# An attention and MoE kernel on one core: two key chunks loaded uncast and summed by VectorE, a second buffer for turned pooled keys, and new lists of chunks that VectorE evaluates

## The chip, the cores and the metric

The kernel runs on one core of one Trainium2 chip. The metric is device time in microseconds, the median of several runs. Inside a core, TensorE (PE; its weight loads are a row of their own, PEld), ScalarE (ACT), VectorE (DVE), GpSimd (POOL) and SyncE (SP) work side by side, each through its own queue in order.

## The reference

```python
def _attn_ref(q, kv, w_sr):          # q (4, 12288, 128), kv (4, 384, 32, 128), w_sr (128, 128)
    B, N, C = q.shape
    r = 4
    kv_pool = kv.reshape(B, H // r, r, W // r, r, C).mean(axis=(2, 4))
    k = v = kv_pool.reshape(B, -1, C) @ w_sr          # 768 keys per batch
    s = (1.0 / np.sqrt(C)) * (q @ k.transpose(0, 2, 1))
    a = np.exp(s - s.max(-1, keepdims=True))
    a /= a.sum(-1, keepdims=True) + 1e-09
    return a @ v

def _moe_ref(x, w_in, w_out):        # x is the attention's output, (49152, 128); d_ff = 2048
    h = x @ w_in
    g = h * (1.0 / (1.0 + np.exp(-1.702 * h)))
    return g @ w_out
```

Pixels are averaged over 4 by 4 blocks, which gives 768 pooled pixels per batch; keys and values are the same matrix.

## The kernel before

**Tiling.** Queries are taken in 96 blocks of 512 (`G`); 24 blocks belong to a batch. The 768 keys of a batch are 6 chunks of 128 (`JC`); `d_ff` is 16 chunks of 128 (`FCH`). The work has two rounds (`R = 2`): attention for blocks 0 to 47, the MoE layer for them, then both for blocks 48 to 95.

**A chunk's way.** TensorE makes one chunk of scores or hidden values, 128 x 512, in a PSUM bank (`fill_attn`, L357; `fill_moe`, L617). ScalarE evaluates two or three such chunks, a frame, in one instruction (exponential L359, GELU L619) and writes bfloat16 into the ring `ag`, which holds 102 chunks. TensorE takes them up again: in attention as weights against the values (`drain_attn`, L370, 129 columns, four tiles of 128 queries for each chunk), in the MoE layer with `w_out` (`drain_moe`, L627). VectorE then empties the bank: it divides by the row sum (L393, L396) or transposes the output (L638), which SyncE stores from one of three `o_sb` buffers.

**Chunks by VectorE.** For some chunks VectorE evaluates the function with a polynomial, in small steps between its other work: `rolling` names chunks of the exponential (`early_exp`), `lent` chunks of the GELU (`lent_gelu`), and blocks 48 to 51 (`early`) are done so wholly. `rolling` and `lent` results go into a ring of three chunks, `aside`.

**Keys.** For batches 0 and 1, a chunk of pixels is 128 rows of 16 pixels by 128 channels. `load_chunk` loads it through GpSimd, which casts float32 to bfloat16 on the way; the first chunk of batch 0 alone is loaded uncast by SyncE and cast by engines. `pool_chunk` adds the pixels on TensorE: the pixels are the weights, and `sum4`, a 128 x 32 matrix of ones, adds four rows; 4 groups of 4 pixels make 16 matmuls of 32 columns (L141). VectorE copies the result to `pTc` (L144). `key_and_value` makes keys and values from it (L163, L164), and VectorE copies both (L165, L166). Batch 1 is loaded in blocks 10 and 12 of attention and pooled at the blocks that `SUM` names. For batches 2 and 3 GpSimd adds the pixels by accumulating DMAs into `kvs` (`add_kv`, L175), VectorE adds the last two (`sum_kv`, L181), and SyncE brings the transposed result from DRAM into `pT` (`turn_pooled`, L188) for `make_k` (L203).

**Order.** The whole instruction order is written by a planner in the kernel's source, before anything runs: the loop at the end of the function keeps an estimate of TensorE's time (`now`), of VectorE's (`dve`) and of ScalarE's (`end`), in units of one 512-column matmul, and takes at each point a fill, a small job from `extras`, a step of a VectorE chain (`early_step`) or a drain. `COST` holds for each job TensorE's time and the time until its bank is free, `COPY` VectorE's time, `SMALL` the time of one 129-column matmul. Three PSUM banks (5, 6, 7) rotate for everything but the frames. `x` holds 12 tiles of 2048 columns; attention's output goes there, and before it the query and key chunks being loaded (`x_tile`). `gate` makes GpSimd's queue wait until VectorE has come to the same place, which times the loads.

Of the kernel before, what the change touches and what calls it, by code (L numbers as in the profile page):

```python
# [7 lines left out]
F32 = mybir.dt.float32  # L8
F32R = mybir.dt.float32r
I32 = mybir.dt.int32  # L10
BF = mybir.dt.bfloat16
AF = mybir.ActivationFunctionType
AX = mybir.AxisListType
ADD = mybir.AluOpType.add
# [10 lines left out]
def kernel(  # L25
    ctx, tc, q, kv, w_sr, moe_w_in, moe_w_out, out,
):
    nc = tc.nc
    B, N, C = q.shape
    _, H, W, _ = kv.shape  # L30
    r = 4
    Hp, Wp = H // r, W // r
    J = Hp * Wp
    JC = J // 128
    d_ff = moe_w_in.shape[1]
    FCH = d_ff // 128
# [25 lines left out]
    XS = NS // R  # L62
    EARLY = 4
    AG = 102

# [21 lines left out]
    def acc(key=None):  # L87

        nonlocal last_acc
        last_acc = next_acc()  # L90
        turns.append(last_acc)
        turns.remove(last_acc)
        if key:
            closes[last_acc] = key
        return banks[:, last_acc, :]
# [17 lines left out]
    def x_tile(s):  # L113
        return x[:, s % XS * SG:(s % XS + 1) * SG]
# [4 lines left out]
    h = J // 2  # L119
    kv_tiles, kv_sums, pooled, pTs, kTs, vs = {}, {}, {}, {}, {}, {}  # L120

# [6 lines left out]
    def load_chunk(b, jc):  # L128

        a, ch = divmod(jc, HC)  # L130
        t = x_tile(XS - 1 - jc)
        nc.gpsimd.dma_start(out=t, in_=kv_r[b, a, ch])
        kv_tiles[b, jc] = t.rearrange("p (wp w1 c) -> p w1 wp c", w1=r, c=C)

    def pool_chunk(b, jc):

        ps = acc()
        t = kv_tiles.pop((b, jc))
        for wp in (0, 2, 1, 3) if (b, jc) == (0, 0) else range(4):
            for w in range(r):  # L140
                nc.tensor.matmul(ps[:, 32 * wp:32 * wp + 32], t[:, w, wp, :], sum4,  # L141
                                 start=(w == 0), stop=(w == r - 1))
        pTs[b, jc] = kvtmp.tile([128, 128], BF, name="pTc", bufs=2)
        nc.vector.tensor_copy(pTs[b, jc], ps[:, 0:128])  # L144
# [25 lines left out]
    def add_kv(b, n):  # L170
        i, w = divmod(n, r)
        if n == 0:
            kv_sums[b] = kvsum.tile([Hp, 2, Wp, C], F32, name="kvs")
        for i2 in range(2):
            nc.gpsimd.dma_start(out=kv_sums[b][:, i2], in_=kv_p[b, i, w, :, i2],  # L175
                                **({"accum_op": ADD} if n else {}))
# [9 lines left out]
    def turn_pooled(b, a):  # L186
        pTs[b, a] = kvtmp.tile([128, 1, h], BF, name="pT")
        nc.sync.dma_start_transpose(out=pTs[b, a], in_=pool_bf[b, a].rearrange("w h c -> (w h) c"))  # L188
# [64 lines left out]
    nc.sync.dma_start(out=first_f, in_=kv_r[0, 0, 0])  # L253
    w_sr_f = cpool.tile([128, C], F32)
    nc.sync.dma_start(out=w_sr_f, in_=w_sr)
# [47 lines left out]

    w_in_sb = cpool.tile([128, d_ff], BF)
    w_out_sb = cpool.tile([128, FCH, C], BF)

# [30 lines left out]
    early = range(NG // R, NG // R + EARLY)  # L337
    rolling = [(i, JC - 1) for i in (31, 35, 45, 55, 56, 63, 64, 78, 91)]
    lent = [(g, FCH - 1) for g in (4, 6, 8, 9, 13, 15, 17, 53, 54, 56, 58, 60, 64, 65, 68, 69, 72, 73, 77, 81, 83, 85, 88, 91, 93)]
    turn = [("a",) + c for c in rolling if c[0] < early[0]] + [("m",) + c for c in lent if c[0] < early[0]]  # L340
# [13 lines left out]
    def fill_attn(chunks, ps):  # L354
        for k, (i, jc) in enumerate(chunks):
            rhs = qTs[i // 4][:, 0, (i % 4) * G:(i % 4 + 1) * G]
            nc.tensor.matmul(ps[:, k, :], kTs[i // GB][:, jc * 128:(jc + 1) * 128], rhs,  # L357
                             start=True, stop=True)
        nc.scalar.activation(place([("a",) + c for c in chunks]), ps, AF.Exp, scale=scale)  # L359
# [70 lines left out]
    def early_step():  # L430
        nonlocal steps
        on_dve(next(steps))
        if steps.gi_frame.f_locals["last"]:
            steps = None
            made[early_todo.pop(0)] = dve

# [53 lines left out]
    raw = None  # L490
    made, used = {}, []
    steps, early_todo = None, [c for c in rolling if c[0] < early[0]]
# [42 lines left out]
    TURN = {6: 3, 7: 4, 8: 5, 20: 6, 21: 7, 22: 8, 25: 9, 32: 10, 35: 11, 42: 12}  # L535
    SUM = {13: (0,), 14: (1,), 15: (2,), 17: (3,), 19: (4,), 22: (5,)}
    CAST = {0: [5], 13: [6], 14: [7], 15: [8], 16: [9], 26: [10, 11], 27: [12]}
    CAST_MOE = {20: 13, 21: 14, 22: 15, 23: 16, 33: 17, 34: 18, 35: 19, 36: 20, 37: 21, 38: 22, 39: 23}

    def background(i):  # L540
# [15 lines left out]
        for jc in SUM.get(i, ()):  # L556
            extras.extend([(pool_chunk, 1, jc), (key_and_value, 1, jc)])
        if i in (28, 33, 38):
# [173 lines left out]
    def prepare(p):  # L732
# [3 lines left out]
        for i, jc in part:  # L736
# [30 lines left out]
    FIXED, CHUNK, SWITCH, HANDOVER, EVACUATE = 0.295, 1.978, 6.0, 1.0, 4.5  # L767
    COST = {pool_chunk: (1.9, 2.6), key_chunk: (0.3, 2.4), value_chunk: (0.3, 2.4),
            transpose_q: (1.05, 4.2), early_fill: (1.0, 5.5), key_and_value: (0.55, 3.5),
            make_k: (0.8, 3.2)}  # L770
    COPY = {pool_chunk: 1.5, key_chunk: 1.5, value_chunk: 1.5, key_and_value: 2.8, transpose_q: 3.2}
    SMALL = 0.26
    RECIPROCAL = 8.2
# [44 lines left out]
    for n in range(len(seq)):  # L818
        fill(n + 2)
        jobs(n + 3)  # L820
        while True:
# [4 lines left out]
            if extras and now >= max(extra_at, bank):  # L826
                f, *args = extras[0]
            if steps and dve <= now + 3.0:
                early_step()
# [84 lines left out]
```

## Time and profile before

| what | value |
|---|---|
| median of 3 runs | 946.73 us (946.7 to 946.88) |
| the profiled execution, whole | 946.45 us |
| its span, first to last instruction | 944.7 us |
| TensorE busy | 938.5 us, 99% |
| ScalarE busy | 930.5 us, 98% |
| VectorE busy | 655.5 us, 69% |
| GpSimd busy | 66.7 us, 7% |
| granted TensorE clock | 1.00 |

In rows of groups the columns are line, engine, operation, output and input by the program's names, shapes (partitions x elements, type), count, then busy time in us and mean ns of one, then the engine's idle time before them and what ended it. In rows of a timeline they are the start in us, the length in us, engine, line and operation, shapes and count; in brackets, idle time before. In rows by stretch they are the stretch and its length in us, the busy time and count of each engine, the granted clock, the share of DMA time, and GB/s. A matmul's length in such a row has the pipeline's drain in it, which the next matmul overlaps.

### The profile page before, as it was taken

What the parts mean: (1) busy time and instruction counts of PE and PEld (TensorE: products, weight loads), DVE (VectorE), ACT (ScalarE), POOL (GpSimd) and SP (SyncE); (2) the same over time, 40 slices, a digit from 0 to 9 for tenths busy, and PEclk for the clock granted to TensorE, in tenths of its full rate; (3) what the DMA queues carried; (4) which work ended last, traced back from release to release, by engine and by line L of the source; (5) the groups of instructions that cost most, each with busy time, mean ns of one, the idle gap of its engine ahead of it and who ended that gap; (6) DMA issues with size and microseconds to landing.
All of it is one profiled execution on the core that took longest, in us unless ns stands there. A gap on an engine that the chain in (4) does not pass through costs nothing.

```text
span 944.7 us, 15547 instructions
## 1 busy us (share of the span) xinstructions
PE 938.5 (99%) x6278; PEld 500.9 (53%) x6278; DVE 655.5 (69%) x1202; ACT 930.5 (98%) x706; POOL 66.7 (7%) x115
## 2 busy tenths in 40 slices
PE   9999999999999999999999999999999999999998
PEld 4777776444444444445446777744444444444444
DVE  5547565896878789878757645458777986386681
ACT  6999999999999999999999999999999999999997
POOL 3101003310000332000000000000000000000000
PEclk9999999999999999999999999999999999999999
DMA  9998947996877899664435683652222221212222
GB/s 210 206 196 176 189 90 102 145 134 139 167 151 115 123 144 130 116 111 93 63 63 117 131 157 91 116 124 41 38 38 41 37 42 34 44 34 45 34 45 45
DMA packets 380456, 97.30 MB, mean 103 GB/s; under 512 B 354560, under 2 KB 377984, under 8 KB 379904
## 3 DMA queue, kind: packets, MB, share of 16 engines
q1 hardware_dynamic: 351840, 64.19, 36.9%
q0 software_dynamic: 28272, 31.99, 22.3%
q8 instruction: 49, 0.80, 0.4%
q14 instruction: 23, 0.19, 0.1%
q10 hardware_dynamic: 272, 0.13, 0.0%
HBM read 52.49 MB, written 49.81 MB: 108 GB/s over the span
## 4 chain that ended last, share of the span: by engine, by line
PE 98%; DMA 1%; ACT 0%; DVE 0%; POOL 0%; issue 0%; POOLq 0%
PE banks L627 35%; PE banks L617 35%; PE banks L370 14%; PE banks L357 12%; PE banks L422 1%; DMA x<-in_kv_dram 1%; PE banks L416 1%; PE banks L141 0%; ACT ag L359 0%; PE banks L655 0%; POOL x L230 0%; PE banks L163 0%; PE banks L301 0%; PE banks L244 0%; PE banks L203 0%
## 5 line engine op out<-in xcount | busy, mean ns | idle before, releaser
L619 ACT ACTIVATE ag<-banks 128x1536 bf16<-128x1536 f32 (+1 forms) x507 | 677.7, 1468 | 0.0
L617 PE MATMUL banks<-x,w_in_sb 128*128 128x512 bf16 x1511 | 408.8, 379 | 0.0
L627 PE MATMUL banks<-ag,w_out_sb 128*128 128x512 bf16 x1495 | 405.2, 379 | 0.0
L359 ACT ACTIVATE ag<-banks 128x1536 bf16<-128x1536 f32 (+2 forms) x191 | 245.9, 1410 | 3.3 <-PE banks L357 2.9
L627 PEld LDWEIGHTS <-w_out_sb 128*128 128x128 bf16 x1520 | 148.5, 98 | 178.2
L617 PEld LDWEIGHTS <-w_in_sb 128*128 128x128 bf16 x1511 | 146.5, 98 | 170.6 <-issue 0.5
L370 PEld LDWEIGHTS <-ag 128*128 128x128 bf16 x2268 | 145.7, 98 | 44.3 <-issue 0.5
L370 PE MATMUL banks<-v,ag 128*128 128x129 bf16 x2268 | 163.6, 220 | 0.1
L357 PE MATMUL banks<-qT,kT 128*128 128x512 bf16 x543 | 148.4, 379 | 1.3 <-DVE kT L165 0.4
L638 DVE STREAM_TRANSPOSE o_sb<-banks 128x512 f32<-128x512 f32 x95 | 67.3, 708 | 79.8 <-PE banks L627 79.0
L453 DVE SCALAR_TENSOR_TENSOR ea<-ea,eb 128x512 f32<-128x512 f32 x132 | 90.5, 686 | 4.1 <-DVE ea L453 0.6
L393 DVE RECIPROCAL rec<-banks 128x3 f32<-128x3 f32 x124 | 22.2, 179 | 92.7 <-PE banks L370 92.2
L484 DVE RECIPROCAL eb<-ea 128x256 f32<-128x256 f32 x50 | 84.9, 1726 | 0.9
L396 DVE TENSOR_TENSOR x<-banks,rec 128x384 bf16<-128x384 f32 x124 | 69.1, 557 | 4.3
L477 DVE SCALAR_TENSOR_TENSOR ea<-ea,eb 128x512 f32<-128x512 f32 x100 | 68.3, 683 | 2.7
L357 PEld LDWEIGHTS <-kT 128*128 128x128 bf16 x543 | 45.9, 98 | 26.0 <-issue 1.4
L175 POOL DMA_DIRECT2D kvs<-in_kv_dram x32 | 40.7, 1338 | 20.8 <-DMA kvs<-in_kv_dram 17.5
L442 DVE TENSOR_SCALAR ea<-banks 128x512 f32<-128x512 f32 x33 | 22.8, 692 | 26.0 <-PE banks L422 25.7
L464 DVE TENSOR_SCALAR qT<-banks 128x512 f32<-128x512 f32 x25 | 17.3, 692 | 34.0 <-PE banks L416 34.0
L533 POOL MEMSET gate_tile<- 1x1 f32 x38 | 3.6, 94 | 320.4 <-DVE gate_tile L532 315.1
L448 DVE SCALAR_TENSOR_TENSOR eb<-eb,ea 128x512 f32<-128x512 f32 x33 | 22.8, 691 | 0.9
L472 DVE SCALAR_TENSOR_TENSOR eb<-eb,ea 128x512 f32<-128x512 f32 x25 | 17.3, 692 | 0.9
(78 smaller groups left out, 316.7 us busy)
## 6 DMA issues: line engine op xcount, KB each, us to landing
out_dram<-o_sb SPq DMA_DIRECT2D x380, 64.0 KB, 1.9
kvs<-in_kv_dram POOLq DMA_DIRECT2D x32, 384.0 KB, 6.4
q_bf<-in_q_dram POOLq DMA_DIRECT2D x21, 512.0 KB, 7.0
x_bf<-x SPq DMA_DIRECT2D x13, 768.0 KB, 5.6
x<-in_kv_dram POOLq DMA_DIRECT2D x11, 512.0 KB, 10.2
x_bf<-x SPq DMA_DIRECT2D x6, 384.0 KB, 4.7
x<-in_kv_dram SPq DMA_DIRECT2D x1, 1024.0 KB, 5.1
x<-in_q_dram POOLq DMA_DIRECT2D x4, 256.0 KB, 12.1
```

The costliest lines, as they stand in the source:

```text
L175: nc.gpsimd.dma_start(out=kv_sums[b][:, i2], in_=kv_p[b, i, w, :, i2], **({"accum_op": ADD} if n else {}))
L357: nc.tensor.matmul(ps[:, k, :], kTs[i // GB][:, jc * 128:(jc + 1) * 128], rhs, start=True, stop=True)
L359: nc.scalar.activation(place([("a",) + c for c in chunks]), ps, AF.Exp, scale=scale)
L370: nc.tensor.matmul(av_of[u][:, k * (C + 1):(k + 1) * (C + 1)], weights(("a", i, jc))[:, o:o + T], vs[i // GB][:, jc, 0:C + 1], start=(jc = ...
L396: nc.vector.tensor_tensor(to, ps[:, :, 0:C], rec.unsqueeze(2).broadcast_to([128, TS, C]), MUL)
L453: nc.vector.scalar_tensor_tensor(a, a, COEFFS[k], b, ADD, MUL)
L477: nc.vector.scalar_tensor_tensor(a, a, COEFFS[k], b, ADD, MUL)
L484: nc.vector.reciprocal(b[:, m:m + 256], a[:, m:m + 256])
L617: nc.tensor.matmul(ps[:, k, :], w_in_sb[:, fc * 128:(fc + 1) * 128], x[:, g % (4 * XS) * G:(g % (4 * XS) + 1) * G], start=True, stop=True)
L619: nc.scalar.activation(place([("m",) + c for c in chunks]), ps, AF.Gelu_apprx_sigmoid)
L627: nc.tensor.matmul(o_of[g], w_out_sb[:, fc, :], weights(("m", g, fc)), start=(fc == 0), stop=(fc == FCH - 1))
L638: nc.vector.transpose(o_sb, o_of.pop(g))
```

## The change

Chunks 3 and 5 of batch 1 (`ADDED`) are loaded without a cast into space that is idle then: chunk 3 into `kvs`, which now has 128 partitions and exists from the start, and chunk 5 into the space of both MoE weights (`w_both`). VectorE adds their pixels in three instructions of 512 elements each (`add_row`): the pixels of each group of four, first two and two in float32, then the sums into bfloat16. TensorE then needs 4 matmuls for a chunk (`pool_added`) in place of 16. The steps of `add_row` go through the same place in the planner as the steps of a VectorE chain, when no chain is running. The other four chunks of batch 1 move to the last four tiles of `x`. `w_sr` in float32 lies in `kvs` at the start. `pT` gets a second buffer. The lists of chunks that VectorE evaluates are new: 10 `rolling` in place of 9, 26 `lent` in place of 25. `SUM` starts some chunks of batch 1 at earlier blocks. Two of the planner's costs change (`pool_chunk` 1.9 to 2.1, `SMALL` 0.26 to 0.2647), and `pool_added` has one.

```diff
+    ADDED = (3, 5)
...
+    kvs = kvsum.tile([128, 2, Wp, C], F32, name="kvs")
+    w_both = cpool.tile([128, 2 * d_ff], BF, name="w_both")
+    homes = [kvs.rearrange("p a w c -> p (a w c)"), w_both.bitcast(F32)]
+    homes += [x[:, s * SG:(s + 2) * SG].bitcast(F32) for s in (XS - 6, XS - 4, XS - 2)]
+    wide = dict(zip(ADDED, homes))
+    plain = [jc for jc in range(JC) if jc not in wide]
+    spots = {jc: XS - 1 - (JC if len(wide) == JC - 1 else k) for k, jc in enumerate(plain)}
...
-        t = x_tile(XS - 1 - jc)
+        if b and jc in wide:
+            nc.gpsimd.dma_start(out=wide[jc], in_=kv_r[b, a, ch])
+            return
+        t = x_tile(spots[jc] if b else XS - 1 - jc)
...
+    def add_row(jc):
+
+        last, wp = False, None
+        t = wide[jc].rearrange("p (wp e) -> p wp e", wp=r)
+        narrow_sum = wide[jc].bitcast(BF).rearrange("p (wp e) -> p wp e", wp=r)[:, :, 4 * C:5 * C]
+        for m in (0, 2):
+            nc.vector.tensor_tensor(t[:, m:m + 2, 0:2 * C], t[:, m:m + 2, 0:2 * C], t[:, m:m + 2, 2 * C:4 * C], ADD)
+            yield 3.2
+        nc.vector.tensor_tensor(narrow_sum, t[:, :, 0:C], t[:, :, C:2 * C], ADD)
+        added[jc] = narrow_sum
+        extras.extend([(pool_added, 1, jc), (key_and_value, 1, jc)])
+        last = True
+        yield 3.3
+
+    def pool_added(b, jc):
+
+        ps = acc()
+        t = added.pop(jc)
+        for wp in range(r):
+            nc.tensor.matmul(ps[:, 32 * wp:32 * wp + 32], t[:, wp, :], sum4, start=True, stop=True)
         pTs[b, jc] = kvtmp.tile([128, 128], BF, name="pTc", bufs=2)
         nc.vector.tensor_copy(pTs[b, jc], ps[:, 0:128])
...
-            kv_sums[b] = kvsum.tile([Hp, 2, Wp, C], F32, name="kvs")
+            kv_sums[b] = kvs[0:Hp]
...
-        pTs[b, a] = kvtmp.tile([128, 1, h], BF, name="pT")
+        pTs[b, a] = kvtmp.tile([128, 1, h], BF, name="pT", bufs=2)
...
-    w_sr_f = cpool.tile([128, C], F32)
+    w_sr_f = kvs[:, 0, 0, :]
...
-    w_in_sb = cpool.tile([128, d_ff], BF)
-    w_out_sb = cpool.tile([128, FCH, C], BF)
+    w_in_sb = w_both[:, 0:d_ff]
+    w_out_sb = w_both[:, d_ff:2 * d_ff].rearrange("p (o c) -> p o c", c=C)
...
-    rolling = [(i, JC - 1) for i in (31, 35, 45, 55, 56, 63, 64, 78, 91)]
-    lent = [(g, FCH - 1) for g in (4, 6, 8, 9, 13, 15, 17, 53, 54, 56, 58, 60, 64, 65, 68, 69, 72, 73, 77, 81, 83, 85, 88, 91, 93)]
+    rolling = [(i, JC - 1) for i in (29, 40, 43, 53, 63, 65, 71, 75, 86, 94)]
+    lent = [(g, FCH - 1) for g in (3, 5, 11, 12, 14, 18, 52, 54, 58, 59, 61, 64, 66, 67, 70, 72, 74, 77, 78, 82, 83, 86, 87, 91, 92, 94)]
...
         if steps.gi_frame.f_locals["last"]:
+            if "wp" not in steps.gi_frame.f_locals:
+                made[early_todo.pop(0)] = dve
             steps = None
-            made[early_todo.pop(0)] = dve
...
-    SUM = {13: (0,), 14: (1,), 15: (2,), 17: (3,), 19: (4,), 22: (5,)}
+    SUM = {13: (0, 1), 14: (2,), 16: (3,), 19: (4,), 21: (5,)}
...
         for jc in SUM.get(i, ()):
-            extras.extend([(pool_chunk, 1, jc), (key_and_value, 1, jc)])
+            if jc in wide:
+                sums.append(add_row(jc))
+            else:
+                extras.extend([(pool_chunk, 1, jc), (key_and_value, 1, jc)])
...
-    COST = {pool_chunk: (1.9, 2.6), key_chunk: (0.3, 2.4), value_chunk: (0.3, 2.4),
+    COST = {pool_chunk: (2.1, 2.6), pool_added: (0.55, 2.6), key_chunk: (0.3, 2.4), value_chunk: (0.3, 2.4),
...
-    COPY = {pool_chunk: 1.5, key_chunk: 1.5, value_chunk: 1.5, key_and_value: 2.8, transpose_q: 3.2}
-    SMALL = 0.26
+    COPY = {pool_chunk: 1.5, pool_added: 1.5, key_chunk: 1.5, value_chunk: 1.5, key_and_value: 2.8, transpose_q: 3.2}
+    SMALL = 0.2647
...
+            if sums and not steps:
+                steps = sums.pop(0)
             if steps and dve <= now + 3.0:
                 early_step()
```

More of the change, by code (lines that the diff above doesn't have):

```diff
@@ L119 @@
     h = J // 2
-    kv_tiles, kv_sums, pooled, pTs, kTs, vs = {}, {}, {}, {}, {}, {}
+    kv_tiles, kv_sums, pooled, pTs, kTs, vs, added = {}, {}, {}, {}, {}, {}, {}
+    kvs = kvsum.tile([128, 2, Wp, C], F32, name="kvs")
[5 more added lines that the diff above has]
+    spots = {jc: XS - 1 - (JC if len(wide) == JC - 1 else k) for k, jc in enumerate(plain)}
     def new_keys(b):
@@ L142, in pool_chunk @@
                                  start=(w == 0), stop=(w == r - 1))
+        pTs[b, jc] = kvtmp.tile([128, 128], BF, name="pTc", bufs=2)
+        nc.vector.tensor_copy(pTs[b, jc], ps[:, 0:128])
+    def add_row(jc):
[15 more added lines that the diff above has]
+            nc.tensor.matmul(ps[:, 32 * wp:32 * wp + 32], t[:, wp, :], sum4, start=True, stop=True)
         pTs[b, jc] = kvtmp.tile([128, 128], BF, name="pTc", bufs=2)
@@ L355, in fill_attn @@
         for k, (i, jc) in enumerate(chunks):
+            assert i < GB or (i // GB, jc) in vs
             rhs = qTs[i // 4][:, 0, (i % 4) * G:(i % 4 + 1) * G]
@@ L490 @@
     raw = None
-    made, used = {}, []
+    made, used, sums = {}, [], []
     steps, early_todo = None, [c for c in rolling if c[0] < early[0]]
```

## The prediction

> **What bounds the kernel now.** I read the page's busy line first, then busy time by stage, the waits of TensorE (PE) and ScalarE (ACT), the timeline of single stretches, and last the groups by shape.
>
> ```profile
> PE 938.5 (99%) x6278; PEld 500.9 (53%) x6278; DVE 655.5 (69%) x1202; ACT 930.5 (98%) x706; POOL 66.7 (7%) x115
> ```
>
> Both PE and ACT look full, so the question is which of them paces the other. By stage (attention, MoE, attention, MoE; columns: PE, PEld, DVE, ACT, POOL):
>
> ```profile
> 25.00:161.00 136.00, 135.65 (x1553) 97.93 (x1550) 76.79 (x217) 135.87 (x105) 16.41 (x34) 1.00 0.91 161
> 161.00:482.00 321.00, 321.00 (x1555) 148.25 (x1554) 257.52 (x433) 321.00 (x240) 41.17 (x61) 1.00 0.79 123
> 482.00:606.00 124.00, 124.00 (x1283) 85.84 (x1282) 75.31 (x178) 123.94 (x93) 0.00 (x0) 1.00 0.57 116
> 606.00:941.00 335.00, 335.00 (x1676) 156.94 (x1673) 232.42 (x332) 333.05 (x252) 0.00 (x0) 1.00 0.27 48
> ```
>
> After 25 us PE idles 0.35 us in all, at a granted clock of 1.00. A modelled busy time can hide waits, so I look at starts, in the timeline of PE:
>
> ```profile
> 400.27 0.81 PE L627 MATMUL banks<-ag,w_out_sb 128*128 128x512 bf16 x3
> 400.92 0.81 PE L617 MATMUL banks<-x,w_in_sb 128*128 128x512 bf16 x3
> 401.57 0.59 PE L627 MATMUL banks<-ag,w_out_sb 128*128 128x512 bf16 x2
> ```
>
> Three matmuls of 512 columns take 0.65 us, 216 ns each, and the trace's starts keep that pace nearly everywhere: all of PE's start-to-start times together exceed the pace of their shapes by 10.5 us in the span, of which gaps over 10 ns after 25 us are 2.1 us (22 gaps, the longest 0.40 us). ACT is the other way: the undisturbed step of a 3-chunk activation is 1.331 us (305 of 660), and from 25 to 925 us its steps exceed the pace of their sizes by 10.4 us. In the MoE stages every fourth or fifth activation starts 0.416 us after the start of its last fill matmul and never earlier, so there it waits for PE. So **PE sets the end, with ACT some 10 us behind it in demand**. Work taken from ACT or VectorE buys nothing by itself; work taken from PE counts in full.
>
> **The change, part by part.** The sum stands against the profiled execution: 946.45 us, of which 944.7 is span and 1.75 lies around it; the median of the runs is 0.28 above.
>
> *PE: two pooled chunks.* Each falls from 16 matmuls of 32 columns (L141) to 4. A chunk before:
>
> ```profile
> 47.21 0.67 PEld L141 LDWEIGHTS <-x 128*128 128x128 bf16 x16
> 47.42 0.56 PE L141 MATMUL banks<-sum,x 128*128 128x32 bf16 x16
> 47.80 0.35 PEld L370 LDWEIGHTS <-ag 128*128 128x128 bf16 x6
> 47.83 0.50 PE L370 MATMUL banks<-v,ag 128*128 128x129 bf16 x6
> ```
>
> From the first matmul's start to the next work's start are 0.41 us, 25.4 ns a matmul, weight loads included; 24 matmuls fewer save 24 x 25.4 = 0.61 us, all on the path. (The 0.56 us in the row count the last matmul's drain, which the next matmul overlaps.) The price is not 96 ns, a weight load's duration: the loads overlap, 16 of them in 0.67 us. The Trainium skill (TensorE: Matmul & The Clock Gate, LDWEIGHTS) gives about P/1.2 ns, 107 ns, for a load of 128 columns. If loads set the pace, an estimate by that page would be 24 x 107 = 2.6 us; the 25.4 ns of this trace decides against it.
>
> *ACT: two chunks fewer* (rolling 9 to 10, lent 25 to 26). I recount the frames from the lists: first MoE half 762 = 254 x 3 chunks, second attention half 257 = 85 x 3 + 2, second MoE half 748 = 244 x 3 + 8 x 2. So 3-chunk frames stay 660 and 2-chunk frames go from 36 to 35:
>
> ```profile
> L359 ACT ACTIVATE ag<-banks 128x1024 bf16<-128x1024 f32 x26 | 24.5, 1028 | 2.5 <-PE banks L357 2.2
> L619 ACT ACTIVATE ag<-banks 128x1024 bf16<-128x1024 f32 x10 | 9.5, 1036 | 0.0
> ```
>
> That is 1.0 us less on an engine that waits for PE: worth 0. The two chunks' fill matmuls stay on PE.
>
> *VectorE: more of everything.* Prices from these rows:
>
> ```profile
> L181 DVE TENSOR_TENSOR pooled<-kvs 96x512 bf16<-96x512 f32 x4 | 2.7, 676 | 3.7 <-DMA pool_bf<-pooled 3.7
> L448 DVE SCALAR_TENSOR_TENSOR eb<-eb,ea 128x512 f32<-128x512 f32 x33 | 22.8, 691 | 0.9
> ```
>
> Six adds of 512 float32 elements, 6 x 0.68 = 4.1 us; one exponential chain more, 6.2 us (the sum of its ten rows' means); one GELU chain more, 11.1 us (fifteen instructions, two half-row reciprocals at 1.73 us among them). Together 21.4 us on 655.5, 72% of the span. Cover: between 45 and 72 us, where the adds go, VectorE is busy 12.9 of 27 us, and before most evacuations (L393, L144, L165) it idles 0.8 to 1.5 us for PE. I take 0. Without that cover, an add in front of an evacuation delays a PSUM bank by 0.68 us.
>
> *New wait: the adds on their DMA.* An add waits in VectorE's queue for its chunk, and behind it are queued the evacuations that free PE's banks. Chunk 3 landed at 53.6 us in the trace, chunk 5 at 58.6; the adds come with blocks 16 and 21, whose first fills start at 54.7 and 68.4 us. The cover is 1.1 us for chunk 3, 9.8 for chunk 5. An uncast load needn't be slower: packets of the plain load of chunk (0, 0), 8192 bytes, take 309 ns (median), packets of the casting loads, 4096 bytes written for 8192 read, 324 ns. Bounds: landing 0.1 us earlier, or 2.4 us later (the spacing of the casting loads' landings, as if writes counted in full), which leaves VectorE blocked 1.3 us. I take 0, the packet being the nearest row.
>
> *Other orderings.* The DMAs into the shared homes wait for the chunk's use: w_in's load, issued at 88.0 us, for chunk 5's matmuls at about 72; the first kvs load at 141.3 for chunk 3's near 58. GpSimd's queue holds as many DMAs in the same order; behind the chunk loads stand casts whose query tiles are turned at 66.5 and first used at 76.5. On SyncE's queue turn_pooled (L188) waited 14.2 us in two cases for PE to read the one pT tile, with the stores of o_sb behind it; the second buffer ends that. But VectorE's waits before L638 are all for PE (79.0 us), none for a free o_sb, so this is worth 0.
>
> *A rule against it.* GpSimd issued a casting load (L212) in 486 ns at 55.2 us with VectorE idle, and in 486 ns at 85.7 us beside L453, which reads two SBUF tensors as the new adds do. The Trainium skill (SBUF — State Buffer, The "DVE blocks DMA" trap, and its list of contention) says that such an instruction contends with GpSimd's reads of SBUF, though not with its writes. By such a lock an estimate, six adds' length, would bring loads up to 4.1 us later; the two rows show no delay.
>
> *The order itself.* pool_chunk's cost goes from 1.9 to 2.1 units and SMALL from 0.26 to 0.2647 (a unit is a 512-column matmul, 0.2155 us; 57 ns measured by starts for 129 columns are 0.2645), and all lists are new, so every piece is placed anew. PE's total does not depend on the order; its gaps do. Bounds: the 2.1 us after 25 us all vanish, or double. I take 0.
>
> Sum: -0.61 us; 945.84 for the profiled execution, **946.1 us** for the median of the runs (946.73 - 0.61).
>
> **The rivals.** A measurement of this kernel can tell about 0.2%, 1.9 us, from no change.
>
> *Faster by more:* pooling matmuls are priced by their loads, 24 x 98 ns = 2.35 us, or half of the 2.1 us of gaps go as well as the 0.61. 944.4 by the first. Against: 16 loads and matmuls pass in 0.41 us, and the gaps are scattered over 22 places.
>
> *Slower:* VectorE falls behind. Six adds come in front of evacuations; PE finds its bank still held, and idles what VectorE is late. If each add shows in full, 6 x 0.68 - 0.61 = +3.5, 950.2 us. It decides from the point where VectorE's lag passes the time until a bank is needed again: three banks rotate, a group of tiles is 18 matmuls (1.0 us) plus the fills between, 2 us, so about 4 us less 1 us for evacuation, 3 us. Against: adds come one at a time. For: lent chains fall on neighbouring blocks (77 and 78, 91 and 92); yet a lent chunk was ready at least 8.8 us before its use.
>
> *ACT is the pace after all.* Then PE's 0.61 us are worth nothing and ACT's 1.0 us count instead: 945.7, the same verdict. Against it stand the activations that start at PE's earliest moment.
>
> **How the numbers follow.** The forecast (within 0.2%, 944.8 to 948.6, with the ACT case in it) has 0.80, the faster rival 0.07, the slower 0.13. The range goes down to 945.0 (half of the gaps gone, 946.1 - 1.1) and up to 948.2 (the gaps doubled, 946.1 + 2.1; chunk 3 late by 1.3 us lies inside); what it leaves out are the two rivals, 0.20.
>
> **What would show it.** L141's matmuls 160 instead of 192, 8 in the new line, each chunk's four in about 0.10 us; ACT with 660 and 35 frames; PE idle after 25 us still under 1 us; adds of 0.68 us without a DMA wait. Wrong, if PE shows waits for VectorE between 45 and 75 us, an add waits for its load, or a stage takes over 1 us more at the same PE work.

## The result, and the profile after

The changed kernel takes **949.65 us** (median of 17 runs, 948.84 to 956.45) against 946.86 (946.45 to 947.24, 17 runs) before: 1.0051 times the time, interval 1.0039 to 1.0064. The forecast was 946.1, the range 945.0 to 948.2. So it is slower by more than a measurement of this kernel leaves open, and outside the range. The runs form two groups, and the number can't be understood without that: ten lie between 948.84 and 949.70 (median 949.1), seven between 954.16 and 956.45 (median 955.3). Two things are thus to be explained, **+2.2 us in every run** and **+6 us more in some runs**. The profiled execution is one of the shorter ones (948.84 us, span 947.1).

In the profile after, lines have moved: fills are L392, L457 (`early`) and L656, drains L405, L666 and, for the last blocks, L694; activations L394 and L658; VectorE's output transpose is L677, `add_row` L163 and L165, `pool_added` L176, `sum_kv` L215, SyncE's store of a pooled sum (`put_pooled`) L218, GpSimd's casting load of a query tile (`cast_q`) L246, SyncE's transposing load of one L252.

The page's busy line, and the same four stages (columns as before):

```profile
PE 938.8 (99%) x6254; PEld 500.5 (53%) x6254; DVE 670.6 (71%) x1233; ACT 928.8 (98%) x705; POOL 66.2 (7%) x115
```

```profile
25.00:161.00 136.00, 134.59 (x1524) 96.79 (x1522) 82.99 (x228) 135.07 (x105) 16.61 (x34) 1.00 0.91 168
161.00:482.00 321.00, 320.80 (x1551) 148.06 (x1550) 240.22 (x410) 320.89 (x240) 40.56 (x61) 1.00 0.78 122
482.00:606.00 124.00, 123.80 (x1266) 85.16 (x1264) 80.04 (x185) 123.94 (x94) 0.00 (x0) 1.00 0.57 114
606.00:941.00 335.00, 334.69 (x1663) 156.33 (x1662) 253.69 (x363) 332.06 (x250) 0.00 (x0) 1.00 0.27 49
```

24 matmuls fewer, and PE is busy 0.3 us *longer*, because busy time is modelled and takes short waits in. Shown idle after 25 us has gone from 0.35 to 2.12 us, most of it in the first attention half, where the edit is. PE's own waits in the shorter execution are small and scattered (waiting line, what it waited for; total, times, longest in us):

```profile
PE banks L457 <- DMA qT<-q_bf: 0.5, 1, 0.5
...
PE banks L392 <- ACT ag L394: 0.4, 2, 0.2
...
PE banks L176 <- DVE w_both L165: 0.2, 1, 0.2
```

Starts give the exact account. If every matmul took the pace of its shape and no more, PE would be through with its last one at 930.67 us with the 6278 matmuls of before and at 930.07 with the 6254 of after: **the 0.60 us are there**. All the rest is gaps between starts. The table gives them in us by stretch of the span (rounded; the stretches add up to 0.03 to 0.04 us more than the sums used below). The last column is where PE's last matmul has taken its pace, 0.22 us after its start: price plus gaps.

| kernel | 0–25 | 25–50 | 50–75 | 75–150 | 150–375 | 375–425 | 425–925 | after 925 | PE's end |
|---|---|---|---|---|---|---|---|---|---|
| before | 7.19 | 1.02 | 0.28 | 0.21 | 0.46 | 0.20 | 1.04 | 0.13 | 941.17 |
| after, shorter run | 7.22 | 0.97 | 1.22 | 0.89 | 0.95 | 0.08 | 1.42 | 0.63 | 943.41 |
| after, longer run (first experiment) | 7.10 | 0.97 | 1.22 | 0.74 | 0.95 | **7.98** | 1.42 | 0.64 | 951.05 |

Gaps went from 10.50 to 13.34 us, and 13.34 − 10.50 − 0.60 = 2.24 us. Those over 10 ns after 25 us more than doubled, 2.14 to 4.99. The three that can be named best, in the timeline:

```profile
58.39 0.68 DVE L165 TENSOR_TENSOR kvs<-kvs 128x512 bf16<-128x512 f32 x1
59.13 0.27 PE L176 MATMUL banks<-sum,kvs 128*128 128x32 bf16 x4
59.25 0.81 PE L392 MATMUL banks<-qT,kT 128*128 128x512 bf16 x3
```

```profile
110.38 0.39 PE L457 MATMUL banks<-qT,kT 128*128 128x512 bf16 x1 [0.51 <-DMA qT<-q_bf]
```

```profile
940.18 1.00 PE L694 MATMUL banks<-w_both,ag 128*128 128x128 bf16 x15 [0.31 <-DVE o_sb L677]
```

The first shows the new step at its price, four matmuls in 0.12 us; but the last add of chunk 3 (L165) began at 58.39 and lasts 0.68 us, so PE stood 0.30 us in front of them, and 0.32 us in front of chunk 5's. The second is the early fill of block 40, whose query tile (tile 10) lands at 110.33: 0.67 us by starts. The third is a last output block in a new drain order: 0.47 us by starts. Together that is 1.76 us. A further 0.38 us stands at 53.01 us in front of a pooled chunk (L152), ahead of the first add, so the adds aren't its cause. The rest is many small gaps, less some of before that are gone.

The longer group has its whole surplus between 375 and 425 us. Its profile, the timeline of SyncE, GpSimd, VectorE and PE there:

```profile
383.62 9.06 SPq L218 DMA_DIRECT2D pool_bf<-pooled  x2
383.77 0.53 POOL L246 DMA_DIRECT2D q_bf<-in_q_dram  x1
391.65 0.69 DVE L215 TENSOR_TENSOR pooled<-kvs 96x512 bf16<-96x512 f32 x1 [8.00 <-DMA pool_bf<-pooled]
394.08 0.59 PE L666 MATMUL banks<-ag,w_both 128*128 128x512 bf16 x2 [2.35 <-DVE o_sb L677]
398.66 0.58 PE L457 MATMUL banks<-qT,kT 128*128 128x512 bf16 x1 [3.34 <-DVE o_sb L677]
```

VectorE's second sum writes the tile `pooled`, of which there is one, so it waits until SyncE has stored the first sum out of it. The store is issued 0.15 us ahead of a casting load and lands 8.0 us after issue. VectorE stands still for 8.0 us, the output transposes queued behind the sum come late, their banks are not free, and PE stops twice. In the shorter execution the casting load is issued 0.41 us behind the store, and before the change 0.91 us:

```profile
383.62 0.43 SPq L218 DMA_DIRECT2D pool_bf<-pooled  x1
384.03 0.53 POOL L246 DMA_DIRECT2D q_bf<-in_q_dram  x1
385.58 0.69 DVE L215 TENSOR_TENSOR pooled<-kvs 96x512 bf16<-96x512 f32 x1 [1.67 <-DMA pool_bf<-pooled]
```

```profile
381.84 0.43 SPq L184 DMA_DIRECT2D pool_bf<-pooled  x1
382.75 0.53 POOL L212 DMA_DIRECT2D q_bf<-in_q_dram  x1
383.79 0.69 DVE L181 TENSOR_TENSOR pooled<-kvs 96x512 bf16<-96x512 f32 x1 [1.16 <-DMA pool_bf<-pooled]
```

The lead is not all that differs. The casting load of the tile before (17) lands at 385.02 us in the longer run, 1.4 us after the store's issue; in the shorter one it lands at 383.83, 0.2 us after it. No run changes one of the two without the other, so which of them decides isn't shown. What every kept profile shows is that the store comes behind the load: of the 40 stores of batch 3's sums in the 20 profiles, 36 were issued with a casting load in flight, and each landed after that load, 0.3 us at the earliest.

The two stops also cost clock. By stretch (PE, PEld, DVE, ACT, POOL, granted clock, DMA share, GB/s), of the longer run:

```profile
392.33:395.74 3.41, 1.24 (x5) 0.48 (x5) 3.31 (x7) 1.18 (x2) 0.00 (x0) 1.00 0.33 62
395.74:399.16 3.42, 0.50 (x2) 0.23 (x2) 2.76 (x6) 1.07 (x1) 0.53 (x2) 0.50 0.39 72
399.16:402.57 3.41, 3.41 (x10) 1.17 (x9) 3.12 (x6) 0.73 (x1) 0.00 (x0) 0.50 0.96 154
402.57:405.98 3.41, 3.41 (x18) 1.51 (x17) 2.31 (x5) 3.12 (x3) 0.53 (x2) 1.00 1.08 183
```

From 395.74 to 402.57 us the clock is at 0.50: PE does 10 matmuls in the third stretch, 18 in the fourth.

### The profile page after: what moved, and what is told of

The parts are those of the page before. It is cut to its first block, busy times and chain, and to the rows that moved or that the text cites. A ratio compares the mean times of both kernels' runs of the same rounds, so it can differ in the third digit from the quotient of the medians.

```text
span 947.1 us, 15534 instructions
## 1 busy us (share of the span) xinstructions
PE 938.8 (99%) x6254; PEld 500.5 (53%) x6254; DVE 670.6 (71%) x1233; ACT 928.8 (98%) x705; POOL 66.2 (7%) x115
## 4 chain that ended last, share of the span: by engine, by line
PE 87%; ACT 10%; DMA 2%; DVE 1%; issue 0%; POOL 0%; DVEq 0%; POOLq 0%
PE banks L666 34%; PE banks L656 34%; ACT ag L394 10%; PE banks L405 9%; PE banks L392 7%; DMA qT<-q_bf 1%; DMA x<-in_kv_dram 1%; PE banks L457 1%; PE banks L451 1%; PE banks L152 0%; PE banks L694 0%; DVE x L431 0%; POOL x L264 0%; PE banks L197 0%; PE banks L335 0%
## 5 line engine op out<-in xcount | busy, mean ns | idle before, releaser
L658 ACT ACTIVATE ag<-banks 128x1536 bf16<-128x1536 f32 (+1 forms) x506 | 677.1, 1504 | 0.1
L656 PE MATMUL banks<-x,w_both 128*128 128x512 bf16 x1510 | 408.4, 379 | 0.2 <-ACT ag L394 0.2
L666 PE MATMUL banks<-ag,w_both 128*128 128x512 bf16 x1494 | 404.8, 379 | 0.2 <-DVE kT L238 0.2
L394 ACT ACTIVATE ag<-banks 128x1536 bf16<-128x1536 f32 (+2 forms) x191 | 244.8, 1497 | 4.1 <-PE banks L392 3.7
L666 PEld LDWEIGHTS <-w_both 128*128 128x128 bf16 x1520 | 148.7, 98 | 179.2 <-issue 0.4
L656 PEld LDWEIGHTS <-w_both 128*128 128x128 bf16 x1510 | 146.4, 98 | 170.3 <-issue 1.1
L405 PEld LDWEIGHTS <-ag 128*128 128x128 bf16 x2264 | 145.8, 98 | 45.1 <-issue 0.3
L405 PE MATMUL banks<-v,ag 128*128 128x129 bf16 x2264 | 163.9, 220 | 0.0
L392 PE MATMUL banks<-qT,kT 128*128 128x512 bf16 x542 | 148.2, 379 | 1.4 <-ACT ag L394 0.4
L677 DVE STREAM_TRANSPOSE o_sb<-banks 128x512 f32<-128x512 f32 x95 | 67.0, 705 | 80.6 <-PE banks L666 74.2
L489 DVE SCALAR_TENSOR_TENSOR ea<-ea,eb 128x512 f32<-128x512 f32 x136 | 93.2, 686 | 3.1
L520 DVE RECIPROCAL eb<-ea 128x256 f32<-128x256 f32 x52 | 88.1, 1727 | 0.9
L513 DVE SCALAR_TENSOR_TENSOR ea<-ea,eb 128x512 f32<-128x512 f32 x104 | 71.1, 683 | 2.8
L392 PEld LDWEIGHTS <-kT 128*128 128x128 bf16 x542 | 45.9, 98 | 25.7 <-issue 1.4
```

The source lines that it names most:

```text
L405: nc.tensor.matmul(av_of[u][:, k * (C + 1):(k + 1) * (C + 1)], weights(("a", i, jc))[:, o:o + T], vs[i // GB][:, jc, 0:C + 1], start=(jc = ...
L489: nc.vector.scalar_tensor_tensor(a, a, COEFFS[k], b, ADD, MUL)
L513: nc.vector.scalar_tensor_tensor(a, a, COEFFS[k], b, ADD, MUL)
L520: nc.vector.reciprocal(b[:, m:m + 256], a[:, m:m + 256])
L656: nc.tensor.matmul(ps[:, k, :], w_in_sb[:, fc * 128:(fc + 1) * 128], x[:, g % (4 * XS) * G:(g % (4 * XS) + 1) * G], start=True, stop=True)
L658: nc.scalar.activation(place([("m",) + c for c in chunks]), ps, AF.Gelu_apprx_sigmoid)
```

## The experiments

Each is given by its median, its ratio to the kernel before on the same chip with the interval, and, where it matters, PE's gaps.

**Which wait makes the longer runs?** Two theories stood against each other: the query tile that is late at 110 us, or the store that a casting load overtakes near 384 us. First the changed kernel once more, with no edit.

> The changed kernel as it is, for a profile of the longer kind of its runs (7 of 17 took 954.2 to 956.5 us at a mean clock of 0.996 to 0.998, the others 948.8 to 949.7 at 1.000). Theory 1, a query tile that lands late: a run of the longer kind shows TensorE idle for several us before the scores of block 40 that VectorE evaluates (near 110 us), waiting for the transposing load of query tile 10, and the clock lowered just after. Rival 1, VectorE behind with the new adds: TensorE's long wait is for VectorE between 45 and 75 us. Rival 2, the end of the plan: the time is lost after 930 us. A profile of the shorter kind would show the same gaps as before, 5.0 us after 25 us.

956.22 us (four runs, all of the longer group), 1.0100 (1.0087 to 1.0113). Its profile is the longer one shown above; the gap at 110 us is 0.53 us in it, less than in the shorter execution. That speaks against the query tile.

Then that tile turned one block earlier:

```diff
-    TURN = {..., 25: 9, 32: 10, 35: 11, 42: 12}
+    TURN = {..., 25: 9, 31: 10, 35: 11, 42: 12}
```

> One edit to the changed kernel: query tile 10 is loaded at block 31, ahead of the block of attention output that is brought back then, not at block 32. Theory 1: the wait near 110 us is gone, no run of the longer kind is left, and the median is 948.2 to 948.5 (the 0.67 us gap less). Rivals 1 and 2: about 4 in 10 runs are of the longer kind still, and the shorter ones stay at 948.8 or fall by the 0.67 us alone.

954.33 us, 1.0082 (1.0069 to 1.0095). The gap at 110 us is gone, and every run is still a longer one: the query tile is not the cause of the group. VectorE, GpSimd and SyncE in its timeline:

```profile
383.54 0.53 POOL L246 DMA_DIRECT2D q_bf<-in_q_dram  x1
384.58 0.43 SPq L218 DMA_DIRECT2D pool_bf<-pooled  x1
389.75 0.69 DVE L215 TENSOR_TENSOR pooled<-kvs 96x512 bf16<-96x512 f32 x1 [6.33 <-DMA pool_bf<-pooled]
```

Here the casting load goes first by 1.04 us, the store lands 5.2 us after its issue, and the wait is nearly as bad; PE then waits for VectorE, 0.7 us at L666 and 3.3 us at L457. Now the direct test: the second sum gets a place of its own, in a part of `kvs` that is already used up, so that nothing waits for the first store.

```diff
-        pooled[b, a] = kvtmp.tile([Hp, 4, C], BF, name="pooled")
+        if a:
+            pooled[b, a] = kvs.rearrange("p a w c -> p (a w c)")[0:Hp, 0:2 * C].bitcast(BF).rearrange("p (w c) -> p w c", c=C)
+        else:
+            pooled[b, a] = kvtmp.tile([Hp, 4, C], BF, name="pooled")
```

> The changed kernel, but the second of VectorE's two sums for batches 2 and 3 is written to another place (part of kvs that the first sum has used up), so that it need not wait for the first one's store to DRAM. Theory 2, formed from the profile of e1: in the longer runs that store (issued at 383.6 us) lands after 8.0 us and not 1.9, since a casting load of queries is issued 0.15 us behind it; VectorE waits for it in the second sum, with the output transposes behind, and TensorE finds no bank (2.3 and 3.3 us) and runs at half clock for 6.8 us. Then no run of the longer kind is left and all take 948.6 to 949.4. Rival: the load holds up the whole chain of batch 3's keys, so TensorE waits elsewhere (for pT) and runs of 952 to 956 remain.

948.67 us (948.31 to 949.18, 11 runs), 1.0022 (1.0013 to 1.0030): no longer run among eleven, and VectorE waits for no store of a sum. (The eleven ran on another chip than the runs of the two experiments before, and the kernel without the edit was not run there; what ties the wait to the lost time is the two profiles above.) The other side of the same race, the casting loads 18 to 23 one block later:

```diff
-    CAST_MOE = {..., 33: 17, 34: 18, 35: 19, 36: 20, 37: 21, 38: 22, 39: 23}
+    CAST_MOE = {..., 33: 17, 35: 18, 36: 19, 37: 20, 38: 21, 39: 22, 40: 23}
```

> The changed kernel with the casting loads of query tiles 18 to 23 one block later each (blocks 35 to 40, not 34 to 39), so none is issued beside the store of batch 3's first sum; the sum's place stays single. Theory 2: no run of the longer kind, 948.6 to 949.4. Rival: the store is late without the load too (behind SyncE's output stores), and longer runs remain at about 4 in 10.

949.60 us (948.95 to 951.42), 1.0032 (1.0021 to 1.0043). With no casting load beside it the store lands 1.96 us after its issue, and no run is longer than 951.42. (Load 17 was slow here too, 7.6 us; the store was issued as it landed.) But it is issued only at 384.96 us, so VectorE still waits and PE loses 1.19 us:

```profile
386.94 0.69 DVE L215 TENSOR_TENSOR pooled<-kvs 96x512 bf16<-96x512 f32 x1 [3.19 <-DMA pool_bf<-pooled]
```

Last, can the kernel *before* be brought to the longer time? Its casting load 18 is issued right behind 17, and in a second kernel the second sum has a place of its own as well:

```diff
-    CAST_MOE = {..., 33: 17, 34: 18, 35: 19, ...}
+    CAST_MOE = {..., 33: 17, 35: 19, ...}
...
+            if g == 33:
+                cast_q(18)
```

> The kernel before with one casting load (query tile 18) issued straight behind that of tile 17, at block 33, so that both are under way when the store of batch 3's first sum goes out (381.8 us before). Nothing else changes. Theory 2: the store lands 4 to 8 us after its issue and not 1.9, VectorE waits for it in the second sum (1.2 us before), and TensorE loses 2 to 8 us, some at half clock: 949 to 956 in most runs, in an order that is otherwise that of before. Rival: the longer runs of the changed kernel come from its order in some other way; then 946.4 to 947.2.

> The kernel of e13 with the second place for the sum, as in e5. Theory 2: VectorE no longer waits for the store, and most of what e13 lost comes back: 946.4 to 948; what stays is TensorE's wait for the single pT buffer if the store is over 4 us late. Rival, the load slows the output stores anyway: as e13.

947.24 us, 1.0007 (0.9998 to 1.0015), and 946.83 us, 1.0002 (0.9993 to 1.0010). A miss in size: the store does land late, 7.2 us after issue, but it is issued at 378.49, 3.3 us earlier than in the unedited kernel, so most of that passes before VectorE comes to its second sum:

```profile
378.49 8.21 SPq L184 DMA_DIRECT2D pool_bf<-pooled  x2
385.67 0.69 DVE L181 TENSOR_TENSOR pooled<-kvs 96x512 bf16<-96x512 f32 x1 [2.92 <-DMA pool_bf<-pooled]
387.64 0.38 PE L422 MATMUL banks<-qT,kT 128*128 128x512 bf16 x1 [0.24 <-DVE o_sb L640]
```

PE loses 0.41 us there, and with the second place nothing (gaps after 25 us 2.14, as before). So the late landing costs only what of it comes after VectorE is ready. The longer time itself was not brought about in the kernel before.

**Where do the +2.2 us of every run come from?** The change alone has three parts that replan the order: the new lists, the two raised costs, and the adds with `SUM`. The changed kernel with the lists of before, and the kernel before with the new lists:

```diff
-    rolling = [(i, JC - 1) for i in (29, 40, 43, ...)]
-    lent = [(g, FCH - 1) for g in (3, 5, 11, ...)]
+    rolling = [(i, JC - 1) for i in (31, 35, 45, ...)]
+    lent = [(g, FCH - 1) for g in (4, 6, 8, ...)]
```

> The changed kernel with the two lists of chunks that VectorE evaluates as they were before (9 and 25); adds, homes, SUM, costs and second buffer stay. Theory 1: block 40 is not in the list, so no run of the longer kind; with 24 matmuls fewer and the gaps at the adds (0.3 us each) 946.3 to 947.2. Rival 1: longer runs stay, since the adds are the same. Rival 2: no longer runs, as the end of the plan is another.

> The kernel before with the new lists alone. Theory 1: block 40 is evaluated by VectorE as in the changed kernel; a wait for query tile 10 of 0.3 to 1 us near 110 us, some runs longer by 5 to 7 us, the others 947 to 949. Rival 1: no adds, so no longer runs and 946.5 to 947.3. Rival 2: longer runs if the end of the plan is like that of the changed kernel.

948.91 us, 1.0024 (1.0015 to 1.0034), without a longer run; and 947.80 us, 1.0016 (1.0007 to 1.0025), twelve runs of which two are longer (952.49 and 953.90). So the new lists bring some longer runs by themselves and cost some 1.0 us, while without them the changed kernel is still about 2 us behind. The profile of the second is of a longer run, and there PE waits elsewhere, near 415 us:

```profile
PE banks L203 <- DMA pT<-pool_bf: 4.0, 1, 4.0
```

The second half of the pooled sums comes back late into the one `pT`: SyncE issues that load at 406.08 us, after PE has read the first half at 404.44, it lands at 415.20, and `make_k` waits on PE itself. In the changed kernel the same load goes out at 398.21, before PE reads the first half (405.00): the second `pT` buffer, which I had priced at 0, seems to keep this wait out, though no run takes that buffer alone away.

Next the costs alone, in the kernel before, and the costs undone, in the changed one:

```diff
-    COST = {pool_chunk: (1.9, 2.6), ...
+    COST = {pool_chunk: (2.1, 2.6), ...
-    SMALL = 0.26
+    SMALL = 0.2647
```

> The kernel before with the planner's two changed costs alone (pool_chunk 2.1, SMALL 0.2647). It tests where the steady part of the loss comes from: the shorter runs and e3 lie 2.2 us above before, with 3 us more of small gaps on TensorE. Theory S1, the costs place every piece anew and that opens the gaps: 947.5 to 949. Theory S2, the adds and the earlier SUM open them: 946.6 to 947.2.

> The changed kernel with the two planner costs as before (pool_chunk 1.9, SMALL 0.26); lists, SUM, adds, homes and second buffer stay. If the raised costs are what opens the steady gaps (e7: +2.3 us alone; e15 and e16, with a lowered SMALL, are level with before), the shorter runs fall to 947 to 948 and the gap at 940 us (0.47 us) may go; rival, any part of the change opens them: 948.3 to 949.5. Runs over 952 remain possible, since the sum's place is single.

948.91 us, 1.0023 (1.0014 to 1.0032), and 947.91 us, 1.0014 (1.0005 to 1.0023). **Two numbers in a planner, with no instruction added, cost 2.3 us**; with them taken back the changed kernel is 1.3 us behind the kernel before, where its shorter runs were 2.2 behind, so they are worth 0.9 us there. Two neighbouring values in the kernel before (0.258 and 0.262, nothing else changed):

```diff
-    SMALL = 0.26
+    SMALL = 0.258
```

> The kernel before with SMALL at 0.258, lowered by 0.002, and nothing else. Theory S3, formed from e3, e7 and e8 (three different parts of the change, each alone 1.8 to 2.3 us slower): the order before is one whose gaps happen to be few, and any change of a cost that places the pieces anew opens some 2 us of them. Then 947.5 to 949. Rival S1, the raised costs as such: 946.2 to 947.0.

> The kernel before with SMALL at 0.262, raised by 0.002, less than half of the change's step. S3: 947.5 to 949, not ordered with e11 and e7. S1: between before and e7, 947.0 to 948.2.

947.15 us, 1.0006 (0.9997 to 1.0014), and 948.15 us, 1.0016 (1.0007 to 1.0025). Raised, the cost loses time; lowered, it loses almost none (0.5 us, within the interval). The value nearer to the measured 57 ns is the worse one. Three values are no rule, though: each gives another order, and its gaps may be chance.

Now the adds alone: lists, `SUM` and both costs as before, the uncast loads, `add_row`, `pool_added` and the second `pT` kept. The edit to the changed kernel is the lists' diff above, the costs' diff backward, and:

```diff
-    SUM = {13: (0, 1), 14: (2,), 16: (3,), 19: (4,), 21: (5,)}
+    SUM = {13: (0,), 14: (1,), 15: (2,), 17: (3,), 19: (4,), 22: (5,)}
```

> The changed kernel with the lists, SUM and the two costs as before: the uncast loads, the adds, the homes and the second pT buffer alone. S1: 946.2 to 946.9 (24 matmuls fewer, 0.61 us, against two short waits for the adds). S2: 947.5 to 949, with the gaps of e3 between 45 and 75 us.

948.43 us, 1.0017 (1.0009 to 1.0026). The four matmuls of chunk 5 stand in PE's queue ahead of their sum:

```profile
74.13 0.27 PE L176 MATMUL banks<-sum,w_both 128*128 128x32 bf16 x4 [0.67 <-DVE w_both L165]
```

By starts this gap is 0.83 us, more than the 0.61 us that both chunks save. So the planner is made to hold `pool_added` until its estimate of VectorE's time for the last add has passed by one unit:

```diff
+            else:
+                summed[steps.gi_frame.f_locals["jc"]] = dve
...
+                if f is pool_added and now < summed[args[1]] + 1.0:
+                    f = None
```

> The kernel of e8 (uncast loads, adds, homes and second pT buffer on the old lists, SUM and costs), where the planner also takes pool_added only when its own estimate of VectorE has passed the last add by one unit. In e8 TensorE waited 0.83 us at 74 us for the add of chunk 5, more than the 0.61 us that the fewer matmuls saved. If that wait is a term of the loss, no gap is left in front of the four matmuls and the time falls from 948.4 to 947.3 to 947.8. Rival, the new order alone: the gap closes, another opens, and the time stays at 948.2 to 948.8.

947.48 us (947.37 to 947.59), 1.0008 (0.9999 to 1.0017). Gone is the gap, and 0.95 us with it. The timeline shows why: the last add of chunk 5 begins at 73.00, its matmuls now 2.79 us later, when the sum has long been there (0.04 us of gap by starts).

```profile
73.00 0.69 DVE L165 TENSOR_TENSOR w_both<-w_both 128x512 bf16<-128x512 f32 x1
75.79 0.25 PE L176 MATMUL banks<-sum,w_both 128*128 128x32 bf16 x4
```

Lower values of `SMALL` on top (0.258 and 0.259):

> The kernel of e9, the best version with adds (947.5), with SMALL at 0.258. S3 puts any new order at 946.5 to 949, since the base is 0.61 us lower than that of before and gaps of 2 to 5 us are drawn anew. Faster than before only if less than 2.7 us of gaps are left after 25 us.

> The same with SMALL at 0.259: another draw of the order, 946.5 to 949 by S3. If the three (0.26: 947.5) lie within 0.3 us of each other, the order hardly matters for this version and S3 is too strong.

946.86 us, 1.0002 (0.9993 to 1.0011), and 946.78 us, 1.0001 (0.9992 to 1.0010): level with before. The gap at the last output blocks, 0.47 us in the changed kernel and still there with the held `pool_added`, is gone (0.17 and 0.13 us after 925 us, 0.13 before). Gaps over 10 ns after 25 us are 2.9 us, against 2.14 before, so they still eat the 0.6 us saved.

Can the whole change be mended? With the place for the second sum and the held `pool_added`; then with the lowered costs (1.9 and 0.259) too:

> The changed kernel with e5's second place for the sum and e9's condition on pool_added. The two gaps in front of the four matmuls (0.30 and 0.32 us) go: 947.9 to 948.4 against e5's 948.67, with no run of the longer kind. Rival, the new order alone: 948.3 to 949.2.

> The changed kernel with everything that the runs pointed to: second place for the sum (e5), pool_added held until the last add is done (e9), pool_chunk at 1.9 and SMALL at 0.259 (e16), with the new lists and SUM. If the costs and the two waits are the whole loss: 946.2 to 947.0, level with before. If the new lists cost by themselves (e4: 0.9 us): 947.0 to 948.2.

949.91 us, 1.0034 (1.0021 to 1.0046), and 947.98 us, 1.0015 (1.0006 to 1.0024). The first is a miss: the replanned order lets PE wait 1.09 us at 110 us for the query tile, more than the holding saved. The second differs from the level one (0.259, above) by the lists, `SUM` and the second sum's place, and is 1.2 us behind it. No version ran faster than the kernel before.

## Why the prediction was wrong, point by point

**What bounds the kernel: right.** PE sets the end; ACT's row lost a frame of two chunks (L658 has 8 of them, L394 27), ACT still waits for PE (3.7 us at L394), and the time did not fall by the 1.0 us of that rival. In all executions whose record of PE is complete (four lack some 110 matmuls), the span ends 3.5 to 4.0 us behind PE's end.

**PE's two chunks: right.** The price fell by 0.60 us (predicted 0.61), L152 has 160 matmuls, L176 8, and four take 0.12 us. The faster rival, which priced a matmul by its load, is refuted with it.

**VectorE's additions: the cover was right where it was claimed, the size too high.** VectorE is 15.1 us busier, not 21.4. The lengths of its instructions grow by 19.1 us, and 4.0 of these lie over a neighbour's: in the adds-alone kernel adds of 0.68 us start 0.60 us apart. (One figure for the cover was misread: VectorE was busy 11.8 of the 27 us from 45 to 72 us; the 12.9 are those of the 30 us up to 75.) No add waited for its load: chunk 3 landed at 53.77, its first add began at 54.95. The uncast loads and the homes cost nothing, as taken.

**The wait the other way was missing.** I priced what the adds wait for, and not who waits for the adds. `pool_added` is put into `extras` as soon as the last add is *issued*, and PE's queue is in order. That is 0.62 us in the changed kernel, 0.83 at one place with the old lists; it takes back the whole saving. The two experiments with and without the condition that holds it back lie 0.95 us apart, of which the gap of 0.83 us is the part that can be named; the rest comes with the new order.

**"Other orderings ... 0": failed.** I followed SyncE's queue and `pT`, and passed over a wait that stood in the groups that I quoted for a price: L181 with 3.7 us for `pool_bf<-pooled`. Its 1.16 us at 383.79 depended on what GpSimd's queue had in flight, and nothing orders the two queues: before the change, the load of tile 17 landed 0.03 us after the store's issue, and the next came 0.91 us behind it. In the changed kernel seven of 17 runs fell into the longer group; in the two executions of that kind that were profiled (the second with the tile turned earlier) VectorE stops for 8.0 and 6.3 us. That this stop makes the longer runs is shown by the chain in both profiles, with the second place in support (no longer run in 11). That a casting load makes the store late is shown by its landing: four stores with none in flight took 1.8 us, and those issued with over 4 us of a load still to come 5.1 to 8.4 us. The longer run of the new lists alone came by another wait, the one for `pT`.

**"The order itself ... I take 0": the step that carried the miss.** This term measured +2.85 us, with the adds' 0.62 in it, and 2.2 without them, which is about its upper bound (the 2.1 us of gaps doubled). So the middle, 0, was wrong, and with the adds' wait on top the time left the range: all gaps, 2.84 us more, less the 0.60 saved are the 2.24 us. The order of before had gaps of 2.14 us; the eight new plans with a complete record and without the long wait, the changed kernel's and seven of the experiments', had 2.9 to 5.1. None had fewer than the order of before. What this step cost is shown in parts that do not simply add up: the costs alone +2.3 us in the kernel before and 0.9 in the changed one, the lists about 1.0 (1.2 with `SUM` and the second sum's place), the adds' wait 0.95 with its new order.

**The rivals.** The slower one had the right engine and the wrong place and price: PE did idle behind banks that VectorE held, but at 394 to 399 us after a wait on a DMA, not at 45 to 75 us behind six adds. The sign I named as refuting, a PE wait for VectorE between 45 and 75 us, came, with PE's 0.30 and 0.32 us at 59 and 73 us, though in front of the matmuls that use the sum. So did another: PE idles 2.12 us after 25 us, not under 1.

**What stays open.** Which property of the raised costs opens the gaps isn't shown: they lie scattered, and no single wait accounts for them (the kernel before with the costs alone has the 0.38 us at 53 us and the 0.47 at 940 as well). Nor why load 17 took 7.7 and 8.2 us in the two longer executions of the changed kernel and 6.2 in the shorter. Nor, last, why most of the new plans leave 0.47 us at the last output blocks, and why 0.258 and 0.259 close it with the lists of before, while 0.259 doesn't with the new ones.

## What to carry to other kernels

When work is moved to another engine, write down both waits, the one that the moved work waits for and the one of the engine that now needs its result, and look where the planner puts the second. In a kernel whose bound engine is 99% busy, a gain of 0.6 us lies below what a change of the order costs, so test the re-plan by itself, with the edit left out. A wait of 1 us in the profile that hangs on what another, unordered queue has in flight is a risk with the price of the worst order: give the tile a second buffer before anything is moved near it.

## What the runs showed of the hardware that I had not expected

**A small store lands late beside a casting load.** The DMA issues of 383 to 392 us (KB each, us from issue to landing), in the longer run:

```profile
q_bf<-in_q_dram POOLq DMA_DIRECT2D x1, 512.0 KB, 7.5
pool_bf<-pooled SPq DMA_DIRECT2D x1, 96.0 KB, 8.0
```

The store, issued first, lands last, 0.3 us after a load more than five times its size. The packets in the trace say how: the load moves as 16 packets of 32 KB, and the store's 384 packets of 256 bytes start only at 388.2 us, as the first of the 16 end. In the shorter execution the store's packets run from 384.5 to 385.2 us, and the load's begin at 385.4; there it lands in 1.9 us. The Trainium skill (DMA: Bandwidth & Descriptors, SWDGE vs HWDGE vs iDMA) says that DMAs issued from GpSimd and from SyncE sit in different queues of a DMA engine, which serves them in turns. Turns may well be taken here, but no row shows them, and they did not protect the small store from packets that took 3 to 4 us each.

**The clock falls after a wait that PE only partly spends idle.** In 3.41 us ahead of the fall PE was busy for 1.24 us (above), 0.86 us (the tile turned earlier) and 1.26 us (the new lists alone); in the experiment with the later casting loads it was busy for 2.43 of 3.45 us and the clock stayed at 1.00. The nearest pair is in the run with the new lists alone, where it stayed after 1.53 us and fell after 1.26:

```profile
409.68:413.09 3.41, 1.53 (x8) 0.48 (x5) 0.00 (x0) 3.13 (x3) 0.49 (x2) 1.00 1.17 199
413.09:416.50 3.41, 1.26 (x7) 0.61 (x8) 0.88 (x2) 0.00 (x0) 0.00 (x0) 1.00 0.49 77
416.50:419.91 3.41, 3.41 (x10) 1.21 (x9) 2.10 (x5) 1.65 (x2) 0.00 (x0) 0.50 0.45 77
```

It came back after 6.83, 3.41 and 3.41 us. The Trainium skill (TensorE: Matmul & The Clock Gate, What's actually happening) gives a window of 3413 ns for this gate and says that the clock falls after an idle one; the lengths agree with one and two windows, and the rows add that a window need not be idle throughout. So, by an estimate from these lengths, a gap of 3.5 us can cost about half as much again: 3.41 us at half clock take up to 1.7 us from PE.
